# Sparse attention and two feed-forward layers on one core: v loaded 64 rows at a time into two buffers

## The chip, the core and the metric

The kernel runs on one core of a Trainium2 chip. TensorE (PE) multiplies matrices out of the on-chip memory into eight accumulator banks, VectorE (DVE), ScalarE (ACT) and GpSimd (POOL) do the element-wise work, and SyncE (SP) issues nearly all transfers between the chip's main memory and the on-chip memory. The engines run on their own and wait for each other by semaphores; each takes its own instructions strictly in order. The metric is the time of one execution in microseconds, as the device measures it.

## The reference

```
scores = q @ k.T / sqrt(64)                      # 4 batches, 8 heads, 576 positions
heads 0-3: keys with 0 <= i - j < 32             # local
heads 4-7: keys j <= i, j % 32 == i % 32         # strided
attn = exp(scores - max);  attn = attn / (sum(attn) + 1e-9)
x = attn @ v                                     # 2304 tokens, 512 wide
h = x @ w_in;   x = (h * sigmoid(1.702 h)) @ w_out      # 512 -> 2048 -> 512
h = x @ w2_in;  y = (h * sigmoid(h)) @ w2_out           # 512 -> 2048 -> 512
```

All inputs are float32, and so is the result.

## The kernel before

The 2304 tokens are cut into eight chunks c = 0 to 7 of 288 tokens, half a batch each. A chunk passes through `attention(c)` and then through the first feed-forward layer in `chunk(c)`. Chunk 7's first layer and the second layer for all tokens follow from 466 us on, under a plan of their own, which the change does not touch.

To use the fast 16-bit products and keep float32 accuracy, an operand is multiplied by a power of two (its scale) and split into a high and a low 16-bit half: the high half is made on ACT (L398) or POOL (L400), the low half on DVE (L405), and each product becomes three (`HI_LO`). A scale needs the sum of squares of its operand: squares are summed on ACT (L504) or DVE (L506) and added up over the partitions by a small product on PE (L419, `scale_sums`). Chunks 0 and 1 multiply q, k and v directly as float32; chunk 0 does its feed-forward so too (L846, L876), while the weights are still coming in.

The weights are 64-bit numbers in memory. `convert` brings in one of 16 blocks of `w_in` or `w_out` (512 KB, `conv_load`, L276), makes three passes on ACT (L444, L281, L285), one on DVE (L289) and one on POOL (L294), and only then can PE use the block. A small product on PE per block (L302) collects its norm. Chunk 0's products on f blocks 0 to 15 follow the blocks as they become ready, and chunk 1 starts when all 16 blocks of `w_out` are done.

For each chunk, `load_v` (L588) brings v into the tile `rv`: three transfers of 63 rows for the local heads into partitions 0 to 62, and for the strided heads either three of 54 rows (even c) or eleven of 18 to 54 rows with pieces of 1 KB (odd c) into partitions 64 and up. There is one `rv`. It is free again when chunk c has split it into `vz` (c > 1), or, for chunks 0 and 1, when their last product with v (L772) has run; the load of the next chunk waits for that on SP, with everything behind it in SP's order.

The softmax of a pair of heads, one local and one strided (`pair`, four per chunk), runs PE scores (L696) - DVE maximum and subtraction (L708, L710) - ACT exp (L713) - DVE sum and reciprocal (L716, L718) - POOL multiplication (L719) - PE transposition (L725) - ACT or DVE copy to `ptt` (L730 to L739). Its row of 64 score columns holds 63 scores, and the last column holds 1e-9 all the time, so that the sum over 64 columns is sum + 1e-9. Five places for the scores (`prt`, NSM), five for `ptt` (NPT), four for the chunk's outgoing tokens (`ts`, NTS, written by L823 and stored by SP at L826) and eight blocks for weights in work (`wm`, NF) are there.

Nothing of this order is found at run time. `Planner` plays the tasks through at build time with a cost for each, gives each engine the ready task of the lowest due time, and writes the instructions in the order of the starts it found. A transfer ends in that plan after a queue time at `rate` (0.27 MB per us here) and 2.0 us more. A buffer count, a cost or a landing time that is changed therefore moves instructions on every engine.

Of the kernel before, what the change touches and what calls it, by code (L numbers as in the profile page):

```python
# [61 lines left out]
class Planner:  # L62
# [32 lines left out]
    def run(self, t=0.0):  # L95
# [17 lines left out]
        while todo:  # L113
# [21 lines left out]
            for e in sorted(engines, key=lambda e: engines[e]):  # L135
# [35 lines left out]
                if isinstance(got.wait, tuple):  # L171
                    link = max(link, got.t1) + got.wait[1] / self.rate
                    end = link + 2.0
                else:
                    end += got.wait
# [8 lines left out]
def attention_moe_moe2_kernel(  # L184
# [133 lines left out]
    NV = 12  # L318
    rv = at.tile([128, NV, 4, D], F32, name="rv")
    qh = at.tile([128, 2, NQ + 16], F16, name="qh")  # L320
    kh = at.tile([128, 2, 2, NK], F16, name="kh")

    vz = at.tile([128, 2, NV * 4, D], F16, name="vz")
    NSM, NPT, NTS, NCV, NF = 5, 5, 4, 2, 8
    prt = at.tile([128, NSM, NLB, 2, W], F32, name="prt")
# [23 lines left out]
    def sel(t, pattern, base, cm):  # L349
        nc.gpsimd.affine_select(  # L350
            out=t, in_=t, pattern=pattern, compare_op=ALU.is_ge, fill=NEG,
            base=base, channel_multiplier=cm)

    nc.vector.memset(rep, 0.0)
    nc.vector.tensor_copy(out=rep[0:32].rearrange("p (j k) -> p j k", j=4), in_=idb[0:32, None, 0:32].to_broadcast([32, 4, 32]))
    nc.vector.memset(rv[0:W, 3 * NLB:NV], 0.0)
    nc.vector.memset(rv[32:W], 0.0)
    nc.scalar.activation(out=tot[:, 0, 0:1], in_=ones[:, 0:1], func=AF.Exp)
    nc.scalar.activation(out=rv[96:128].rearrange("p n h d -> p (n h) d"), in_=ones[96:128, None, 0:D].to_broadcast([32, 4 * NV, D]),
                         func=AF.Copy, scale=0.0)  # L360
# [3 lines left out]
    nc.gpsimd.memset(mk[0:32, 4, 0, 0:31], NEG)  # L364
    sel(mk[0:32, 0], [[0, NLB], [1, W]], 0, -1)
    sel(mk[0:32, 0], [[0, NLB], [-1, W]], 31, 1)
    for z, r, d in ((2, R9, 0), (3, R18, R9)):
# [5 lines left out]
    for i in range(2):  # L373
        nc.gpsimd.memset(rk[64:128, i, 0:KO], 0.0)
    nc.gpsimd.memset(qh[:, :, NQ:NQ + 16], 0.0)
    nc.gpsimd.memset(prt[:, :, :, :, W - 1], 1e-9)


    P = Planner({"ps": range(8), "rq": [0], "rk": range(2), "rv": [0], "qh": [0],
                 "k0": [0], "k1": [0], "vz": [0], "x1": [0], "sl": range(NSM), "pt": range(NPT), "t": range(NTS),  # L380
                 "cv": range(NCV), "f": range(NF)} | {f"g{f}": [0] for f in range(KF)}, 0.27)

# [189 lines left out]
    def attention(c, b):  # L572
        s = c % 2
        tab = ATT0 if c == 0 else ATT1 if c == 1 else ATT
        rqb, rvb = P.buf("rq"), P.buf("rv")

# [11 lines left out]
        def load_v(on):  # L588
            vc = v[c].rearrange("p i h d -> p i (h d)")
            to = rv.rearrange("p n h d -> p n (h d)")  # L590
            parts = [(0, slice(3 * j, 3 * j + 3), vc[32 * j + 1:32 * j + W, 0:NLB]) for j in range(3)]
            if s == 0:
                parts += [(W, slice(4 * z, 4 * z + 4), vc[27 * z:27 * z + 54, NLB:NLB + 4]) for z in range(3)]
            else:
                parts += [(W + R18 * u, slice(n, n + 7 * m - 6, 7),
                           vc[R18 * r:R18 * (r + w), NLB + i:NLB + i + 3 * m - 2:3])
                          for n, m, u, i, r, w in ((0, 2, 0, 0, 0, 3), (1, 2, 0, 0, 3, 3), (2, 1, 0, 0, 6, 1), (2, 1, 1, 1, 0, 2),
                                                   (3, 1, 0, 1, 2, 3), (4, 1, 0, 1, 5, 2), (4, 1, 2, 2, 0, 1), (5, 1, 0, 2, 1, 3),
                                                   (6, 1, 0, 2, 4, 3), (9, 1, 0, 4, 2, 3), (10, 1, 0, 4, 4, 3))]
            for p0, n0, x in parts:  # L600
                nc.sync.dma_start(out=to[p0:p0 + x.shape[0], n0], in_=x)
        kv = P.add({"SP": 0.4 + 0.5 * s}, b + tab["load"][1], load_v, (), [rvb], wait=("dma", 1.2))


        if c > 0:
            sq = [*([square(c, b + tab["square"][0], NQ, 0, lambda: rq, [kq], [rqb])] if c > 1 else []),
                  *[square(c, b + tab["square"][1], 128 * NV, 1 + 3 * z, lambda z=z: rv.rearrange("p b h d -> p (b h d)")[
                      :, 128 * NV * z:128 * NV * (z + 1)], [kv], [rvb]) for z in range(2)]]
# [27 lines left out]
        if c > 1:  # L636
            qhb, vzb = P.buf("qh"), P.buf("vz")
            k_q = hi_lo(b + tab["split"][0], NQ, lambda: qh[:, 0, 0:NQ], lambda: qh[:, 1, 0:NQ], lambda: rq, lambda: sc_t[c]["q"],
                        [k_sc], [qhb], [rqb])
            split_k(c, b + tab["split"][1])  # L640
            k_v = []
            for t in range(2):
                rvv = rv.rearrange("p b h d -> p (b h) d")[:, 2 * NV * t:2 * NV * (t + 1)]
# [10 lines left out]
        def pair(i):  # L654
# [6 lines left out]
            def scores(on):  # L661
# [45 lines left out]
            for g in range(2):  # L707
# [40 lines left out]
        def times_v(r):  # L748
# [4 lines left out]
            def mm(on):  # L753
                seq = [[], []]
                for g in range(2):
                    rows = slice(W * g, W * g + W)
                    for e, j, c0, n in BLOCKS[s] if g else [(e, j, 0, 0) for e in range(NLB) for j in range(3)]:
                        for x, (y, z) in enumerate(HI_LO if c > 1 else HI_LO[:1]):
                            for hh in range(2):
# [631 lines left out]
```

## Time and profile before

| | |
|---|---|
| median of 3 runs | 851.86 us (850.16 to 853.89) |
| profiled execution, its own time | 851.69 us |
| its span, first to last instruction | 849.9 us |
| PE busy | 814.9 us (96%) |
| DVE, ACT, POOL busy | 618.2, 530.4, 383.5 us |
| PE idle | 35.0 us, of it 25.4 before 125.3 us |
| moved by transfers | 156.83 MB, 185 GB/s |

Times in all rows are us from the span's start. A row of a timeline ends with the idle time of the engine just before it and what ended that. A granted clock of 1.00 is TensorE's upper level, 2.4 GHz, and 0.50 its lower, 1.2 GHz; 0.78 for a stretch is a mean of the two.

### The profile page before, as it was taken

What the parts mean: (1) busy time and instruction counts of PE and PEld (TensorE: products, weight loads), DVE (VectorE), ACT (ScalarE), POOL (GpSimd) and SP (SyncE); (2) the same over time, 40 slices, a digit from 0 to 9 for tenths busy, and PEclk for the clock granted to TensorE, in tenths of its full rate; (3) what the DMA queues carried; (4) which work ended last, traced back from release to release, by engine and by line L of the source; (5) the groups of instructions that cost most, each with busy time, mean ns of one, the idle gap of its engine ahead of it and who ended that gap; (6) DMA issues with size and microseconds to landing.
All of it is one profiled execution on the core that took longest, in us unless ns stands there. A gap on an engine that the chain in (4) does not pass through costs nothing.

```text
span 849.9 us, 24691 instructions
## 1 busy us (share of the span) xinstructions
PE 814.9 (96%) x10112; PEld 682.7 (80%) x10112; DVE 618.2 (73%) x1118; ACT 530.4 (62%) x980; POOL 383.5 (45%) x396
## 2 busy tenths in 40 slices
PE   4989889999999999999999999999999999999997
PEld 2766567877877878877788878888889988888886
DVE  5357679977786989978652537789888799878742
ACT  5788569569879788886761515455554676645510
POOL 4346755342432556734410543778877543211110
PEclk9999989999999999999999999999999999999999
DMA  8968443155474686663310743776666898657501
GB/s 230 267 217 276 121 125 107 39 164 190 140 221 151 216 288 196 197 220 122 109 45 24 305 163 109 234 230 223 224 212 219 299 295 306 235 173 231 180 26 50
DMA packets 90545, 156.83 MB, mean 185 GB/s; under 512 B 9096, under 2 KB 48848, under 8 KB 90432
## 3 DMA queue, kind: packets, MB, share of 16 engines
q1 hardware_dynamic: 90112, 154.67, 56.3%
q8 instruction: 79, 1.29, 0.7%
q10 hardware_dynamic: 320, 0.59, 0.3%
q14 instruction: 34, 0.28, 0.1%
HBM read 101.74 MB, written 53.48 MB: 183 GB/s over the span
## 4 chain that ended last, share of the span: by engine, by line
PE 68%; DMA 15%; DVE 5%; ACT 5%; POOL 3%; issue 2%; SPq 1%; DVEq 0%; POOLq 0%; ACTq 0%
PE aps L1161 10%; PE aps L1272 8%; DMA rv<-in_v_dram 7%; PE hps L1161 5%; PE aps L849 4%; PE gps L1161 4%; PE gps L880 4%; PE aps L880 4%; PE hps L1272 4%; PE gps L1272 4%; DMA regB<-in_moe_w_in_dram 2%; PE gps L849 2%; PE hps L880 2%; PE hps L849 2%; PE gps L1024 1%
## 5 line engine op out<-in xcount | busy, mean ns | idle before, releaser
L1161 PEld LDWEIGHTS <-wf 128*128 128x128 f16 x1680 | 150.6, 98 | 15.3
L1272 PEld LDWEIGHTS <-wf 128*128 128x128 f16 x1512 | 147.6, 98 | 18.6 <-issue 1.1
L849 PEld LDWEIGHTS <-regA 128*128 128x128 f16 x1152 | 112.5, 98 | 29.3 <-issue 0.3
L880 PEld LDWEIGHTS <-regB 128*128 128x128 f16 x1152 | 110.2, 98 | 26.7
L977 POOL TENSOR_TENSOR tt<-tt 128x256 f32<-128x256 f32 (+2 forms) x84 | 75.2, 905 | 45.4 <-ACT tt L1173 12.1
L849 PE MATMUL aps<-x,regA 128*128 128x288 f16 x624 | 83.0, 286 | 0.0
L294 POOL TENSOR_TENSOR wm<-wm 128x512 int32<-128x512 int32 x32 | 45.9, 1438 | 68.1 <-DVE wm L289 63.0
L972 ACT ACTIVATE wf<-tt,xsg 128x512 f16<-128x512 f32 x87 | 58.0, 713 | 26.0 <-PE hps L1272 6.7
L984 DVE SCALAR_TENSOR_TENSOR wf<-tt,xsg,wf 128x512 f16<-128x512 f32 x87 | 70.5, 857 | 0.0
L880 PE MATMUL aps<-g,regB 128*128 128x288 f16 x432 | 58.9, 286 | 0.0
L719 POOL TENSOR_TENSOR prt<-prt,sus 128x378 f32<-128x378 f32 x32 | 29.1, 916 | 55.6 <-DVE sus L718 50.0
L1272 PE MATMUL aps<-regA,wf 128*128 128x256 f16 x456 | 53.2, 273 | 0.1
L1161 PE MATMUL aps<-xfa,wf 128*128 128x256 f16 (+1 forms) x528 | 53.1, 256 | 0.0
L880 PE MATMUL gps<-g,regB 128*128 128x288 f16 x384 | 52.2, 286 | 0.0
L880 PE MATMUL hps<-g,regB 128*128 128x288 f16 x336 | 44.7, 286 | 0.0
L1173 ACT ACTIVATE tt<-tt 128x512 f32<-128x512 f32 x39 | 24.4, 625 | 30.5 <-DVE tt L1168 30.3
L849 PE MATMUL gps<-x,regA 128*128 128x288 f16 x288 | 39.2, 286 | 0.0
L1161 PE MATMUL aps<-g,wf 128*128 128x256 f16 x324 | 38.8, 273 | 0.0
L972 ACT ACTIVATE wf<-regB,xsg 128x512 f16<-128x512 f32 x39 | 26.8, 713 | 18.9 <-DMA regB<-g_scratch 5.9
L405 DVE SCALAR_TENSOR_TENSOR g<-aps,sg,g 128x288 f16<-128x288 f32 x52 | 26.2, 512 | 17.0 <-ACT g L398 16.7
L1272 PE MATMUL aps<-regB,wf 128*128 128x256 f16 x312 | 37.0, 273 | 0.0
L289 DVE SCALAR_TENSOR_TENSOR wm<-wm,aps 128x512 int32<-128x512 int32 x35 | 23.8, 681 | 15.5 <-ACT aps L285 15.5
(335 smaller groups left out, 1906.4 us busy)
## 6 DMA issues: line engine op xcount, KB each, us to landing
tt<-g_scratch SPq DMA_DIRECT2D x76, 256.0 KB
g_scratch<-tt SPq DMA_DIRECT2D x64, 256.0 KB
w<-in_moe_w_out_dram SPq DMA_DIRECT2D x24, 512.0 KB
regB<-in_moe_w_in_dram SPq DMA_DIRECT2D x16, 512.0 KB
w<-in_moe_w_in_dram SPq DMA_DIRECT2D x16, 512.0 KB
w_scratch<-wm SPq DMA_DIRECT2D x32, 256.0 KB
regB<-g_scratch SPq DMA_DIRECT2D x32, 256.0 KB
wf<-in_factors SPq DMA_DIRECT2D x8, 896.0 KB
```

The lines of the kernel that those rows point to most:

```text
L289: nc.vector.scalar_tensor_tensor(out=mi, in0=mi, scalar=3, in1=ri, op0=ALU.logical_shift_left, op1=ALU.bitwise_or)
L294: nc.gpsimd.tensor_tensor(out=di, in0=m.bitcast(I32), in1=di, op=ALU.add)
L405: dve_t(n), prio, lambda on: nc.vector.scalar_tensor_tensor(out=lo(), in0=src(), scalar=s(), in1=hi(), op0=ALU.mult, op1=ALU.subtract),
L719: kno = P.add({"POOL": 1.0}, t + 8, lambda on: nc.gpsimd.tensor_tensor(out=sets(N), in0=sets(N), in1=wide(sus[:, sl.idx], 2 * NLB), op=ALU ...
L849: nc.tensor.matmul(o, lhsT=pvA[:, f, x, kk, :], rhs=x1[:, y, kk, :], start=(i == 0), stop=(i == 3 * KD - 1))
L880: nc.tensor.matmul(o, lhsT=pvB[:, f, u, dt * 128:(dt + 1) * 128], rhs=g1[:, w, f, :], start=(f == 0 and j == 0), stop=(f == KF - 1 and j = ...
L972: nc.scalar.activation(out=out, in_=in_, func=AF.Copy, scale=s)
L977: return P.add({e: x for e, x in any_add(n).items() if e in by}, prio, lambda on: (nc.gpsimd if on == "POOL" else nc.vector).tensor_tensor ...
L984: dve_t(n), prio, lambda on: nc.vector.scalar_tensor_tensor(out=lo(), in0=src(), scalar=s(), in1=hi(), op0=ALU.mult, op1=ALU.subtract),
L1161: nc.tensor.matmul(place(b, f), lhsT=wf[:, nf * g + f, x, wa, 128 * kk:128 * kk + 128], rhs=rhs.rearrange("p (h t) -> p h t", h=2) if n2 = ...
L1173: return P.add(act_t(512), t + 5, lambda on: nc.scalar.activation(out=sl(b), in_=sl(b), func=AF.Silu), after, (), [b], tab="silu")
L1272: nc.tensor.matmul(bank(b)[:, 256 * half:256 * half + 256], lhsT=fb[:, x, a, 128 * f:128 * f + 128], rhs=wt[:, 4 * p + f, z, wi, :], start ...
```

## The change

Below, v2 is the load of v for chunk 2, and so on.

- `rv` becomes two buffers, `rv0` for even and `rv1` for odd chunks, each with its own place in the plan. v of chunk c+1 can be loaded while chunk c's is in use.
- The local loads, and the strided ones of even chunks, take 64 rows instead of 63 and 54. The additional rows carry values that meet a zero probability; the masks move by the one column. In odd chunks the eleven small transfers stay as they were.
- The scores take all 64 columns; the column with 1e-9 goes, and DVE adds 1e-9 to the six sums of a pair just before the reciprocal, 32 instructions more.
- NSM and NPT go from 5 to 4, NTS from 4 to 3, NF from 8 to 7.
- In the plan the queue rate goes from 0.27 to 0.30, a load of v costs SP 1.0 us (even) or 3.0 us (odd) instead of 0.4 and 0.9, and it lands 1.0 or 3.0 us later than its queue time says.
- At the start, DVE clears the last quarter of both buffers (2 x 768 elements) and the lower half of `rv1`; ACT's clearing of 32 rows and POOL's filling of the column go.

```diff
-                    end = link + 2.0
+                    end = link + 2.0 + sum(got.wait[2:])
...
-    rv = at.tile([128, NV, 4, D], F32, name="rv")
+    rv = at.tile([128, 2, NV, 4, D], F32, name="rv")
...
-    NSM, NPT, NTS, NCV, NF = 5, 5, 4, 2, 8
+    NSM, NPT, NTS, NCV, NF = 4, 4, 3, 2, 7
...
-    nc.vector.memset(rv[0:W, 3 * NLB:NV], 0.0)
-    nc.vector.memset(rv[32:W], 0.0)
+    nc.vector.memset(rv[0:W, :, 3 * NLB:NV], 0.0)
+    nc.vector.memset(rv[W:128, 1], 0.0)
     nc.scalar.activation(out=tot[:, 0, 0:1], in_=ones[:, 0:1], func=AF.Exp)
-    nc.scalar.activation(out=rv[96:128].rearrange("p n h d -> p (n h) d"), in_=ones[96:128, None, 0:D].to_broadcast([32, 4 * NV, D]),
-                         func=AF.Copy, scale=0.0)
...
-    nc.gpsimd.memset(prt[:, :, :, :, W - 1], 1e-9)
...
-    P = Planner({"ps": range(8), "rq": [0], "rk": range(2), "rv": [0], "qh": [0],
+    P = Planner({"ps": range(8), "rq": [0], "rk": range(2), "rv0": [0], "rv1": [0], "qh": [0],
...
-        rqb, rvb = P.buf("rq"), P.buf("rv")
+        rqb, rvb = P.buf("rq"), P.buf(f"rv{s}")
...
-            parts = [(0, slice(3 * j, 3 * j + 3), vc[32 * j + 1:32 * j + W, 0:NLB]) for j in range(3)]
+            parts = [(0, slice(3 * j, 3 * j + 3), vc[32 * j:32 * j + W, 0:NLB]) for j in range(3)]
             if s == 0:
-                parts += [(W, slice(4 * z, 4 * z + 4), vc[27 * z:27 * z + 54, NLB:NLB + 4]) for z in range(3)]
+                parts += [(W, slice(4 * z, 4 * z + 4), vc[27 * z:27 * z + W, NLB:NLB + 4]) for z in range(3)]
...
-        kv = P.add({"SP": 0.4 + 0.5 * s}, b + tab["load"][1], load_v, (), [rvb], wait=("dma", 1.2))
+        kv = P.add({"SP": 1.0 + 2.0 * s}, b + tab["load"][1], load_v, (), [rvb], wait=("dma", 1.2, 1.0 + 2.0 * s))
...
-            N = W - 1
+            N = W
...
-            krc = P.add({"DVE": 0.15}, t + 5.1, lambda on: nc.vector.reciprocal(out=sus[:, sl.idx], in_=sus[:, sl.idx]), [ku], (), [sl])
+
+            def inverse(on):
+                nc.vector.tensor_scalar(out=sus[:, sl.idx], in0=sus[:, sl.idx], scalar1=1e-9, scalar2=None, op0=ALU.add)
+                nc.vector.reciprocal(out=sus[:, sl.idx], in_=sus[:, sl.idx])
+            krc = P.add({"DVE": 0.22}, t + 5.1, inverse, [ku], (), [sl])
```

First place: SP's transfers while the weights come in. `regB<-in_moe_w_in` and `regB<-in_moe_w_out` are blocks of weights; `rv` of three and three rows belongs to an even chunk, the one with the small pieces to an odd one. Before, from the blocks 8 to 11 of `w_in` on:

```order
L276 DMA regB<-in_moe_w_in_dram 128x1024 x4
L601 DMA rv<-in_v_dram 63x768 x3
L601 DMA rv<-in_v_dram 54x2x256 x2
L601 DMA rv<-in_v_dram 18x256
L601 DMA rv<-in_v_dram 36x256
L601 DMA rv<-in_v_dram 54x256
L601 DMA rv<-in_v_dram 36x256
L601 DMA rv<-in_v_dram 18x256
L601 DMA rv<-in_v_dram 54x256 x4
L276 DMA regB<-in_moe_w_in_dram 128x1024 x4
L276 DMA regB<-in_moe_w_out_dram 128x1024 x6
```

After, from the end of the load of v1 on:

```order
L598 DMA rv<-in_v_dram 54x256 x4
L276 DMA w_103<-in_moe_w_out_dram 128x1024 x2
L576 DMA rq<-in_q_dram 64x1152
L577 DMA rq<-in_q_dram 64x1152
L276 DMA regB<-in_moe_w_in_dram 128x1024 x4
L598 DMA rv<-in_v_dram 64x768 x3
L598 DMA rv<-in_v_dram 64x1024 x3
L276 DMA regB<-in_moe_w_in_dram 128x1024 x4
L276 DMA regB<-in_moe_w_out_dram 128x1024 x7
```

The load of v1 has moved up past six blocks of weights and q of chunk 1, and v2, which stood behind the 13th block of `w_out`, now stands between blocks 11 and 12 of `w_in`.

Second place: DVE where v2 is squared (`jv,tot<-rv`). Before, among the low halves of `w_in` (L405), late in chunk 0's feed-forward:

```order
L405 SCALAR_TENSOR_TENSOR regA<-regA,s 128x512
L800 SCALAR_TENSOR_TENSOR x_75<-aps,x1s,x_75 128x288 x2
L405 SCALAR_TENSOR_TENSOR regA<-regA,s 128x512
L289 SCALAR_TENSOR_TENSOR wm<-wm,gps 128x512
L405 SCALAR_TENSOR_TENSOR regA<-regA,s 128x512 x2
L506 SCALAR_TENSOR_TENSOR jv,tot<-rv 128x1536
L405 SCALAR_TENSOR_TENSOR regA<-regA,s 128x512
L257 TENSOR_SCALAR a<-aps 128x3
L259 TENSOR_SCALAR t<-a 128x3
L263 RECIPROCAL s<-t 128x3
```

After, where the last blocks of `w_in` are converted (`wm<-wm` is L289, `nms` and `prt` belong to chunk 1's softmax):

```order
L289 SCALAR_TENSOR_TENSOR wm<-wm,hps 128x512
L705 TENSOR_REDUCE nms<-hps 128x3
L705 TENSOR_REDUCE nms<-gps 128x3
L707 TENSOR_TENSOR prt<-hps,nms 128x3x64
L707 TENSOR_TENSOR prt<-gps,nms 128x3x64
L503 SCALAR_TENSOR_TENSOR jv,tot<-rv 128x1536
L289 SCALAR_TENSOR_TENSOR wm<-wm,hps 128x512
L503 SCALAR_TENSOR_TENSOR jv,tot<-rv 128x1536
L289 SCALAR_TENSOR_TENSOR wm<-wm,gps 128x512
L733 TENSOR_SCALAR ptt<-aps 128x384
```

The square that was one instruction on DVE and one on ACT is now two on DVE, and two conversions stand behind and between them.

Third place: SP after v of chunk 3. `x_scratch<-ts` are the stores of chunk 0's outgoing tokens, `rk` is k for chunks 4 and 5. Before:

```order
L601 DMA rv<-in_v_dram 54x256 x4
L826 DMA x_scratch<-ts 128x288 x3
L562 DMA rk<-in_k_dram 64x1280
L563 DMA rk<-in_k_dram 64x1152
L826 DMA x_scratch<-ts 128x288 x2
L276 DMA w_103<-in_moe_w_in_dram 128x1024
```

After:

```order
L598 DMA rv<-in_v_dram 54x256 x4
L559 DMA rk<-in_k_dram 64x1280
L560 DMA rk<-in_k_dram 64x1152
L598 DMA rv<-in_v_dram 64x768 x3
L598 DMA rv<-in_v_dram 64x1024 x3
L559 DMA rk<-in_k_dram 64x1280
L560 DMA rk<-in_k_dram 64x1152
L827 DMA x_scratch<-ts 128x288 x5
L276 DMA w_103<-in_moe_w_in_dram 128x1024
```

The load of v4 and both loads of k now stand ahead of the first store.

## Rows read from the trace of the kernel before

**Rows 1.** The page: busy time of each engine, and TensorE's granted clock in 40 slices.
```profile
PE 814.9 (96%) x10112; PEld 682.7 (80%) x10112; DVE 618.2 (73%) x1118; ACT 530.4 (62%) x980; POOL 383.5 (45%) x396
PEclk9999989999999999999999999999999999999999
```

**Rows 2.** Busy time by stretch: length, five engines, granted clock, DMA share, GB/s.
```profile
0.00:79.70 79.70, 63.28 (x840) 48.18 (x840) 40.67 (x97) 58.14 (x105) 36.12 (x50) 0.98 0.84 241
79.70:109.70 30.00, 21.48 (x182) 15.79 (x182) 20.92 (x29) 19.16 (x33) 20.67 (x15) 0.94 0.57 168
109.70:125.30 15.60, 15.10 (x125) 11.76 (x126) 14.17 (x18) 11.88 (x16) 10.55 (x7) 0.78 0.39 113
125.30:500.00 374.70, 370.70 (x5667) 298.45 (x5666) 282.57 (x586) 268.65 (x539) 157.43 (x153) 1.00 0.50 164
500.00:850.00 350.00, 344.38 (x3302) 308.48 (x3300) 259.86 (x391) 172.53 (x289) 158.75 (x173) 1.00 0.60 198
```

**Rows 3.** Waits of TensorE up to 130 us: total us, times, longest us.
```profile
PE hps L302 <- POOL regB L294: 5.9, 3, 2.8
PE aps L772 <- DMA rv<-in_v_dram: 5.6, 3, 4.3
PE aps L419 <- ACT jk L504: 2.6, 1, 2.6
```

**Rows 4.** Timeline, 108 to 111 us: start, us, instruction, [idle before <- releaser].
```profile
108.11 1.48 ACT L504 ACTIVATE jk<-rv 128x1536 uint8<-128x1536 f32 x1 [3.83 <-DMA rv<-in_v_dram]
108.82 1.76 DVE L506 SCALAR_TENSOR_TENSOR jv<-rv 128x1536 uint8<-128x1536 f32 x1 [3.64 <-DMA rv<-in_v_dram]
109.73 0.45 PE L419 MATMUL aps<-tot,ones 128*128 128x1 f32 x2 [2.64 <-ACT jk L504]
110.65 0.58 PE L419 MATMUL aps<-tot,ones 128*128 128x1 f32 x2 [0.46 <-DVE jv L506]
```

**Rows 5.** Timeline of SyncE's transfers up to 130 us.
```profile
37.24 15.87 SPq L601 DMA_DIRECT2D rv<-in_v_dram  x14
53.20 1.77 SPq L276 DMA_DIRECT2D regB<-in_moe_w_in_dram  x4
95.96 2.17 SPq L601 DMA_DIRECT2D rv<-in_v_dram  x6
```

**Rows 6.** The chain of waits up to 130 us: start, us, what.
```profile
9.73 13.50 DMA rv<-in_v_dram
97.76 11.04 DMA rv<-in_v_dram
```

**Rows 7.** Busy time by stretch, while 64-row loads of q and k run.
```profile
74.40:82.40 8.00, 6.23 (x107) 4.45 (x107) 7.02 (x7) 4.70 (x10) 5.38 (x5) 1.00 0.97 255
```

**Rows 8.** Timeline of TensorE, 62 to 66 us.
```profile
62.17 0.61 PE L302 MATMUL hps<-regA 128*128 128x128 bf16 x4 [2.09 <-POOL regA L294]
62.57 3.63 PE L846 MATMUL gps<-x,regA 128*128 128x288 f32 x8
```

**Rows 9.** Timeline of GpSimd, 64 to 88 us.
```profile
64.66 2.50 POOL L294 TENSOR_TENSOR regA<-wm,regA 128x512 int32<-128x512 int32 x2 [0.38 <-DVE wm L289]
79.62 8.34 POOL L294 TENSOR_TENSOR regB<-wm,regB 128x512 int32<-128x512 int32 x4 [1.90 <-DVE wm L289]
```

**Rows 10.** A small VectorE operation: min/median/max ns.
```profile
L264 DVE TENSOR_SCALAR s<-s x13: 153/169/666, 61.5 to 520.1; 128x1 f32<-128x1 f32 x5, 128x3 f32<-128x3 f32 x4, 128x2 f32<-128x2 f32 x4
```

**Rows 11.** Instructions on rv, min/median/max ns.
```profile
L506 DVE SCALAR_TENSOR_TENSOR jv<-rv x7: 1711/1758/2423, 54.1 to 366.2; 128x1536 uint8<-128x1536 f32 x7
L356 DVE MEMSET rv<- x1: 698/698/698, 1.2 to 1.2; 64x768 f32 x1
```

**Rows 12.** Timeline of VectorE, 135 to 137 us.
```profile
135.27 1.97 DVE L405 SCALAR_TENSOR_TENSOR kh<-rk,s,kh 128x1280 f16<-128x1280 f32 x1
```

**Rows 13.** The chain of waits at 690 us.
```profile
690.38 3.50 DMA g_scratch<-tt
```

**Rows 14.** Waits of TensorE, 130 to 500 us.
```profile
PE aps L725 <- POOL prt L719: 2.7, 3, 1.4
```

More of the change, by code (lines that the diff above doesn't have):

```diff
@@ L363, in attention_moe_moe2_kernel @@
     nc.gpsimd.memset(mk[0:32, 3, :, 54:W], NEG)
-    nc.gpsimd.memset(mk[0:32, 4, 0, 0:31], NEG)
-    sel(mk[0:32, 0], [[0, NLB], [1, W]], 0, -1)
-    sel(mk[0:32, 0], [[0, NLB], [-1, W]], 31, 1)
+    nc.gpsimd.memset(mk[0:32, 4, 0, 0:32], NEG)
+    sel(mk[0:32, 0], [[0, NLB], [1, W]], -1, -1)
+    sel(mk[0:32, 0], [[0, NLB], [-1, W]], 32, 1)
     for z, r, d in ((2, R9, 0), (3, R18, R9)):
@@ L375, in attention_moe_moe2_kernel @@
     nc.gpsimd.memset(qh[:, :, NQ:NQ + 16], 0.0)
-    nc.gpsimd.memset(prt[:, :, :, :, W - 1], 1e-9)
-    P = Planner({"ps": range(8), "rq": [0], "rk": range(2), "rv": [0], "qh": [0],
+    P = Planner({"ps": range(8), "rq": [0], "rk": range(2), "rv0": [0], "rv1": [0], "qh": [0],
                  "k0": [0], "k1": [0], "vz": [0], "x1": [0], "sl": range(NSM), "pt": range(NPT), "t": range(NTS),
-                 "cv": range(NCV), "f": range(NF)} | {f"g{f}": [0] for f in range(KF)}, 0.27)
+                 "cv": range(NCV), "f": range(NF)} | {f"g{f}": [0] for f in range(KF)}, 0.30)
     def start(n):
@@ L589, in load_v @@
             vc = v[c].rearrange("p i h d -> p i (h d)")
-            to = rv.rearrange("p n h d -> p n (h d)")
-            parts = [(0, slice(3 * j, 3 * j + 3), vc[32 * j + 1:32 * j + W, 0:NLB]) for j in range(3)]
+            to = rv[:, s].rearrange("p n h d -> p n (h d)")
+            parts = [(0, slice(3 * j, 3 * j + 3), vc[32 * j:32 * j + W, 0:NLB]) for j in range(3)]
             if s == 0:
-                parts += [(W, slice(4 * z, 4 * z + 4), vc[27 * z:27 * z + 54, NLB:NLB + 4]) for z in range(3)]
+                parts += [(W, slice(4 * z, 4 * z + 4), vc[27 * z:27 * z + W, NLB:NLB + 4]) for z in range(3)]
             else:
@@ L601, in load_v @@
                 nc.sync.dma_start(out=to[p0:p0 + x.shape[0], n0], in_=x)
-        kv = P.add({"SP": 0.4 + 0.5 * s}, b + tab["load"][1], load_v, (), [rvb], wait=("dma", 1.2))
+        kv = P.add({"SP": 1.0 + 2.0 * s}, b + tab["load"][1], load_v, (), [rvb], wait=("dma", 1.2, 1.0 + 2.0 * s))
         if c > 0:
             sq = [*([square(c, b + tab["square"][0], NQ, 0, lambda: rq, [kq], [rqb])] if c > 1 else []),
-                  *[square(c, b + tab["square"][1], 128 * NV, 1 + 3 * z, lambda z=z: rv.rearrange("p b h d -> p (b h d)")[
+                  *[square(c, b + tab["square"][1], 128 * NV, 1 + 3 * z, lambda z=z: rv[:, s].rearrange("p b h d -> p (b h d)")[
                       :, 128 * NV * z:128 * NV * (z + 1)], [kv], [rvb]) for z in range(2)]]
@@ L642, in attention @@
             for t in range(2):
-                rvv = rv.rearrange("p b h d -> p (b h) d")[:, 2 * NV * t:2 * NV * (t + 1)]
+                rvv = rv[:, s].rearrange("p b h d -> p (b h) d")[:, 2 * NV * t:2 * NV * (t + 1)]
                 z = [vz[:, a, 2 * NV * t:2 * NV * (t + 1)] for a in range(2)]
@@ L678, in scores @@
                                     o = LQ * e + 32 * j
-                                    seq[0].append((L[32 * j:32 * j + 32, W * e:W * e + W - 1], qx[:, o:o + 32], kx[:, o + 1:o + W], last))
+                                    seq[0].append((L[32 * j:32 * j + 32, W * e:W * e + W], qx[:, o:o + 32], kx[:, o:o + W], last))
                                 continue
@@ L767, in mm @@
                                     o, pt, u = o[:, LQ * e + 32 * j:LQ * e + 32 * j + 32], pt[:, m:m + 32], 3 * j + e
-                                seq[g].append((o, vz[rows, y, 4 * u + h, :] if c > 1 else rv[rows, u, h, :], pt, x == 0, x == 2 or c < 2))
+                                seq[g].append((o, vz[rows, y, 4 * u + h, :] if c > 1 else rv[rows, s, u, h, :], pt, x == 0, x == 2 or c < 2))
                 for n in range(0, max(len(x) for x in seq), 2):
```

## The prediction

> **What bounds the kernel now.** I read the page first: PE is busy 814.9 of 849.9 us, so 35.0 us is all that idle time can give, and a lower clock is the only other loss [rows 1]. The second look was the busy time by stretch [rows 2]. It splits the idle time: 16.4 us up to 79.7, 8.5 from there to 109.7, 0.5 up to 125.3, 4.0 up to 500 and 5.6 behind. From 125.3 to 500 us PE is 99% busy at the full clock, and what remains behind 500 is not touched by the change. So the case is decided before 125.3 us, while the weights come in. The granted clock is 0.94 in the second stretch and 0.78 in the third; the missing 6% of 30.0 us and 22% of 15.6 us are 1.8 and 3.4 us that PE lost there at the lower level, next to 9.0 us of idle time. The stretch from 79.7 to 125.3 thus holds 14.2 us that PE does not need.
>
> Third I read who ended PE's waits [rows 3]: 5.9 us for converted blocks of w_out, 5.6 for the first load of v, 2.6 for a square on ACT, the last at one place. The timeline there [rows 4] shows what the reader is to see: ACT stood 3.83 us and DVE 3.64 us, both for v2; behind their squares PE waited 2.64 and 0.46 us for the scale of chunk 2. That is 3.1 us in which ready products of chunk 0 stood behind the scale product in PE's order, and right behind it the clock was low: 3.4 us more. v2 had been issued only at 95.96 [rows 5], and the chain gives 11.04 us of its time to it [rows 6].
>
> **The change, part by part.** The sum is made against the profiled execution's own 851.69 us (849.9 us of span and 1.8 around it), 0.2 us under the median.
>
> *v2 early.* With a second buffer and its new place v2 goes out between blocks 11 and 12 of w_in, ahead of the four blocks that went out at 53.20, so some 43 us sooner [rows 5], since its buffer is free once chunk 0's products are done. DVE now squares it among the last conversions of w_in, and nothing waits for it at 104 us. That removes 3.1 us of wait and the low clock behind it, 3.4 us: 6.5 us. What is late next there is the conversion of w_out, for which PE waited 5.9 us elsewhere in the stretch; those waits I leave as they are. Bounds: 3.1 us if another pause at this place brings the clock down all the same, 14.2 us if the conversions, no longer held up by ACT's and DVE's stand, run ahead of PE through the whole stretch.
>
> *v2 ahead of weights.* Blocks 12 to 15 of w_in now land behind v2, and PE already waited 2.09 us for block 12 and then ran at the lower clock (eight products in 3.63 us) [rows 8]. v2 is 3 x 192 KB + 3 x 256 KB = 1.38 MB. The nearest row for 64-row loads is the stretch in which q and k of chunks 2 and 3 come in, 255 GB/s at a DMA share of 0.97 [rows 7]: 5.4 us. Against it stands the better shape of the first load: the chain waits 13.50 us for it [rows 6], while up to 79.7 us the queue moved 241 GB/s [rows 2]. If all that goes before block 12 moves at 255, it is through 5.5% sooner, 3.4 us of 62. That leaves +2.0 us, and I take it; the bounds are 0 (the first load's gain is as large as its price) and 5.4 (it gains nothing).
>
> The row that speaks for 255 GB/s is a stretch of loads of 64 rows that keep the engines 0.97 busy. The Trainium skill, "SBUF — State Buffer", section "Door 1: The DMA port swizzle", says that 64 partitions reach only 8 of the 16 ports on the memory's side, and gives 196 GB/s for them. By that figure, an estimate, v2 costs 7.0 us instead of 5.4 and the sum is 1.6 us worse. The trace's 255 GB/s is above the page's figure, so the row decides.
>
> *Squares next to conversions.* Two squares of v2 on DVE at 1.76 us [rows 11] now run while POOL converts the last blocks of w_in. One conversion on POOL takes 1.25 us alone and 2.09 us where DVE squares q and k: two in 2.50 us, four in 8.34 [rows 9]. Three conversions (blocks 10 to 12) at 0.84 us more are 2.5 us. The squares also stand in DVE's order ahead of blocks 11 and 12; behind them wait the conversions of these blocks, POOL's additions and PE's products on them. But PE is then waiting for block 12 anyway, which lands behind v2: the two prices overlap, and I add nothing for this one, with 0 and 2.5 us as ends.
>
> The rows show POOL at 2.09 us against 1.25. The Trainium skill, "SBUF — State Buffer", section "Who interferes with whom", makes it harder: a VectorE instruction with two inputs in this memory and a GpSimd instruction that reads it hold a shared interface one at a time, and the second one waits for the whole of the first. By that rule each square could cost a conversion its full 1.76 us, 3.5 us in all, and if none of it overlapped the forecast would be that much later. Rows of before do not show so much.
>
> *v1 early, v0 faster.* v1's fourteen transfers took SP 15.87 us and held up blocks 12 to 15 of w_in, issued at 53.20 [rows 5]; now they stand ahead of blocks 8 to 11 too. Their 1.2 MB are 4.7 us at 255 GB/s; less 5.5% of some 43 us, 2.4, that is 2.3 us later. PE then comes to block 12, which waits behind v2 in any case: I take 0, from 0 to 2.3. PE's 5.6 us wait for v0 [rows 3] shrinks, but what PE wins there it waits again at block 12: 0, with -5.6 as the end.
>
> *The rest.* 32 additions on DVE at 0.17 us [rows 10] are 5.4 us over some 400 us, beside PE's work and on an engine busy 73% of the span: 0, at most 0.5. One score column more, and 378 elements becoming 384, are under 2% of operations that end nothing. The start has one more clearing of 0.70 us [rows 11] ahead of PE's first product, hidden in the wait for v0; without that cover, 0.7 us. Four softmax places are as many as a chunk has pairs; PE waited 2.7 us in all for a normalised pair from 130 to 500 us [rows 14]. I take no change, -2.7 to +3.
>
> Sum: 851.7 - 6.5 + 2.0 = 847.2 us. On the median's scale that is 847.4.
>
> **The rivals.**
>
> *Given back.* PE arrives earlier and waits for the next late thing, the blocks of w_out (5.9 us of waits already [rows 3]) or block 12. For it: POOL was busy 20.7 of 30.0 us from 79.7 on [rows 2], and what chunk 2 needs (high and low halves of q, k, v) now falls into that same stretch. Against it: ACT and DVE stood still for 3.7 us exactly there. If v2 costs its full 5.4 us, 851.7 - 6.5 + 5.4 = 850.6; 850 to 853.
>
> *Slower: stores behind loads.* The stores of chunk 0's tokens now stand on SP behind v4 and the second load of k, which waits until DVE has made the low half of the k before it (1.97 us at 135.27 [rows 12]). There are three `ts` places for four columns of tokens, so ACT's fourth copy waits for a store to land; 3.50 us is one store's time [rows 13]. Behind that copy stand ACT's gelus and high halves, and PE runs out of banks. For it: the order, and the fourth place is gone in all seven chunks of this plan. Against it: in the order ACT has nine operations between the first copy and the fourth. If each chunk lost half a store's time, 1.75 us, it is 7 x 1.75 = 12.3 us, and 847.2 + 12.3 = 859.5; from 0.65 us a chunk on it takes back the whole 4.5 us. I put it at 856 to 860.
>
> *More than the wait.* With ACT and DVE never stopped, w_out's conversions finish ahead of PE, and most of the 14.2 us closes: with 2.0 us of price, 839.5; 838 to 843. Against it: POOL's load in that stretch.
>
> **How the numbers follow.** Forecast 0.50 (own range 845 to 851, since its cost may be 0 to 5.4), given back 0.20, slower 0.13, more 0.17. Anything within 0.5% (4.3 us) is about what a measurement of this kernel cannot tell from no change, so faster means under 847.6. A little over half of the forecast's chance lies there, 0.29, and all of the last rival's: 0.46. The rest of the forecast and the giving back are the same: 0.41. Slower 0.13. The range goes from 840 to 855: it leaves out the lower end of the largest gain and the slower rival.
>
> **What would show it.** In the profile after: no wait of ACT, DVE or PE for v around 104 to 110 us, no low clock behind it, and chunk 1's first 16-bit products (L849 before) starting some 4 us before 125.3. v2 issued before 60 us. PE's wait for block 12 of w_in longer by about 2 us, and POOL's additions of blocks 11 to 13 near 2 us. From there to 500 us PE 99% busy. I am wrong if PE's wait for blocks of w_in grows by more than 5 us, if the time from 79.7 us to chunk 1's start stays at 45 us, or if new waits of PE stand beside stores of `ts` behind 125 us.

## The result and the profile after

The changed kernel takes 857.5 us, median of 6 runs (854.4 to 858.9), against 851.0 for the kernel before in the runs beside it (848.8 to 853.9, 6 runs). The ratio is 1.0071, with a 95% interval of 1.0046 to 1.0096: some 6 us slower. I had forecast 847.4 in a range of 840 to 855 and given "slower" 0.13. The profiled execution of after took 857.71 us, 6.0 more than that of before.

The same rows of the page of after; they answer to [rows 1]:

```profile
PE 820.3 (96%) x10112; PEld 684.6 (80%) x10112; DVE 619.6 (72%) x1144; ACT 528.3 (62%) x981; POOL 390.5 (46%) x395
PEclk9989999999999999999999999999999999999999
```

PE is 5.4 us longer busy, and its idle time is the same (35.3 us). More busy time for nearly the same products means lower clock, so idle time and clock have to be read together, by stretch. The busy time by stretch of after, which answers to [rows 2]:

```profile
0.00:79.70 79.70, 64.89 (x744) 49.16 (x745) 42.32 (x101) 54.25 (x100) 35.36 (x46) 0.94 0.87 254
79.70:109.70 30.00, 25.71 (x282) 18.89 (x280) 26.91 (x39) 22.80 (x41) 26.26 (x19) 0.94 0.66 192
109.70:125.30 15.60, 13.16 (x137) 9.74 (x138) 14.64 (x24) 10.33 (x16) 12.30 (x9) 1.00 0.75 188
125.30:500.00 374.70, 366.52 (x5608) 293.77 (x5606) 273.54 (x589) 267.91 (x536) 155.30 (x149) 1.00 0.48 154
```

Idle time plus the share lost to the clock, before and after:

| stretch | before | after | difference |
|---|---|---|---|
| 0 to 79.7 us | 16.4 + 1.6 = 18.0 | 14.8 + 4.8 = 19.6 | +1.6 |
| 79.7 to 125.3 | 9.0 + 5.2 = 14.2 | 6.7 + 1.8 = 8.5 | -5.7 |
| 125.3 to 500 | 4.0 + 0 = 4.0 | 8.2 + 1.7 = 9.9 | +5.9 |

(The 1.7 of the last row is half of 3.41 us at the lower level, too short to show in the two digits of its clock.) That is 1.8 of the 6.0 us. Up to 3.0 more lie at the very start, where these two traces record no clock, before 28.0 us in one and 30.0 us in the other. The timeline of TensorE of after shows the level there by the length of eight equal products:

```profile
26.11 4.08 PE L847 MATMUL aps<-x,regA 128*128 128x288 f32 x8
30.26 2.16 PE L847 MATMUL hps<-x,regA 128*128 128x288 f32 x8
```

Before, the first eight of them started at 28.97 us and took 2.15 us. Of the runs below, sq5_behind_ts has the same start as after, and its trace does record the level there. Behind 3.4 us at the upper level, the busy time by stretch shows a granted clock of 0.50:

```profile
13.80:30.70 16.90, 14.02 (x197) 11.71 (x198) 8.17 (x18) 12.30 (x24) 9.69 (x9) 0.50 1.02 286
```

If the level was the lower one all the way up to the recorded part, after did 20.7 us of work at it and before 14.7, and half of the difference is 3.0 us. The last 1.2 us I can't assign.

So the gain that I forecast is there (-5.7), and two losses stand against it: one up to 80 us, larger than forecast, and one behind 125 us, where I had said that nothing would change. The waits of TensorE in after, up to 130 us and then from 130 to 500 us, answer to [rows 3, 14]:

```profile
PE hps L302 <- POOL regB L294: 6.7, 7, 2.1
PE hps L661 <- DVE rep L355: 6.5, 1, 6.5
PE aps L661 <- ACT g L855: 2.8, 1, 2.8
PE gps L693 <- DMA rq<-in_q_dram: 1.0, 1, 1.0
...
PE hps L693 <- DMA rq<-in_q_dram: 0.9, 1, 0.9
PE aps L302 <- POOL regA L294: 0.8, 1, 0.8
PE aps L773 <- DMA rv<-in_v_dram: 0.3, 2, 0.2
...
PE gps L850 <- ACT ts L824: 2.2, 1, 2.2
PE hps L693 <- issue: 2.1, 1, 2.1
```

The 5.6 us for v0 are down to 0.3, the 2.6 us for a square of v2 are gone. New are 1.9 us for q of chunk 1, 2.8 us for a bank that ACT empties only behind its pass over block 12 of w_in, 2.2 us for a copy to `ts` and 2.1 us for scores.

The pause of 2.2 us is the largest piece behind 125 us, and the low clock (142.6 to 146.1 us) follows it. The timelines of SyncE, ScalarE and TensorE of after around it:

```profile
134.18 0.47 SPq L559 DMA_DIRECT2D rk<-in_k_dram  x1
135.38 7.10 SPq L827 DMA_DIRECT2D x_scratch<-ts  x4
...
139.70 1.27 ACT L501 ACTIVATE jk<-rk 128x1280 uint8<-128x1280 f32 x1 [1.15 <-DMA rk<-in_k_dram]
140.97 0.48 ACT L395 ACTIVATE g<-aps,sg 128x288 f16<-128x288 f32 x1
141.35 0.49 ACT L395 ACTIVATE g<-gps,sg 128x288 f16<-128x288 f32 x1
141.73 0.41 ACT L824 ACTIVATE ts<-gps 128x288 f32<-128x288 f32 x1
...
142.19 2.64 PE L850 MATMUL gps<-x,regA 128*128 128x288 f16 x12 [2.20 <-ACT ts L824]
```

PE wants the bank that ACT's fourth copy of chunk 0's tokens empties. ACT stands 1.15 us for k of chunk 5 (call it k5), issued only at 134.18, squares it, makes two high halves, and only then copies. But the copy also needs one of three `ts` places, and the first store, issued at 135.38 behind k5, landed at 141.15. The copy started at 141.73, so two causes end 0.6 us apart, and the trace names only the later one. That called for experiments on each alone and on both.

### The profile page after: what moved, and what is told of

Its sections match the earlier page's. It is cut to its first block, busy times and chain, and to the rows that moved or that the text cites. A ratio compares the mean times of both kernels' runs of the same rounds, so it can differ in the third digit from the quotient of the medians.

```text
span 855.6 us, 24711 instructions
## 1 busy us (share of the span) xinstructions
PE 820.3 (96%) x10112; PEld 684.6 (80%) x10112; DVE 619.6 (72%) x1144; ACT 528.3 (62%) x981; POOL 390.5 (46%) x395
## 4 chain that ended last, share of the span: by engine, by line
PE 61%; DMA 11%; DVE 11%; ACT 8%; POOL 4%; issue 3%; SPq 1%; DVEq 0%; ACTq 0%; POOLq 0%
PE aps L1162 10%; PE aps L1273 8%; PE hps L1162 5%; PE gps L1162 4%; PE hps L1273 4%; PE gps L1273 4%; PE aps L850 3%; PE hps L881 3%; DMA rv<-in_v_dram 3%; DMA rq<-in_q_dram 2%; PE aps L881 2%; PE gps L881 2%; PE hps L850 2%; PE gps L850 2%; POOL wm L294 2%
## 5 line engine op out<-in xcount | busy, mean ns | idle before, releaser
L294 POOL TENSOR_TENSOR wm<-wm 128x512 int32<-128x512 int32 x32 | 48.2, 1507 | 83.7 <-DVE wm L289 78.9
L881 PE MATMUL aps<-g,regB 128*128 128x288 f16 x576 | 78.5, 286 | 0.0
L850 PE MATMUL aps<-x,regA 128*128 128x288 f16 x552 | 74.5, 288 | 0.0
L720 POOL TENSOR_TENSOR prt<-prt,sus 128x384 f32<-128x384 f32 x32 | 29.2, 917 | 46.7 <-DVE sus L718 34.5
L850 PE MATMUL hps<-x,regA 128*128 128x288 f16 x336 | 45.6, 286 | 0.5 <-DVE g L402 0.5
L402 DVE SCALAR_TENSOR_TENSOR g<-aps,sg,g 128x288 f16<-128x288 f32 x46 | 23.1, 512 | 24.1 <-ACT g L395 24.0
L850 PE MATMUL gps<-x,regA 128*128 128x288 f16 x264 | 36.8, 291 | 2.2 <-ACT ts L824 2.2
L294 POOL TENSOR_TENSOR regA<-wm,regA 128x512 int32<-128x512 int32 x16 | 21.6, 1359 | 32.1 <-DVE wm L289 31.1
```

The lines of the kernel that those rows point to most:

```text
L294: nc.gpsimd.tensor_tensor(out=di, in0=m.bitcast(I32), in1=di, op=ALU.add)
L402: dve_t(n), prio, lambda on: nc.vector.scalar_tensor_tensor(out=lo(), in0=src(), scalar=s(), in1=hi(), op0=ALU.mult, op1=ALU.subtract),
L850: nc.tensor.matmul(o, lhsT=pvA[:, f, x, kk, :], rhs=x1[:, y, kk, :], start=(i == 0), stop=(i == 3 * KD - 1))
L881: nc.tensor.matmul(o, lhsT=pvB[:, f, u, dt * 128:(dt + 1) * 128], rhs=g1[:, w, f, :], start=(f == 0 and j == 0), stop=(f == KF - 1 and j = ...
```

## The experiments

Several edits move single instructions of the finished plan and leave all others in their order:

```diff
+        for k, to in self.moves:
+            k.t0 = to.t0 + 1e-3
         for k in sorted(self.tasks, key=lambda k: (k.t0, k.seq)):
             k.fn(k.on)
```

Ratios are to the kernel before, on the same chip; the changed kernel itself has 1.0071.

**The square of k5 behind the fourth copy.**

```diff
+                if x == 5:
+                    P.moves.append((sq[-1], ts_copy))      # the last of chunk 0's copies
```

> One instruction moves against the changed kernel: ACT's square of k of chunk 5 (127 lines of order below nothing else) stands behind ACT's fourth copy of chunk 0's tokens instead of three places ahead of it. Theory A (ACT was held by this square, whose load was issued only at 134.18 us): the high halves and the copy no longer wait for that load, PE's pause of 2.20 us at 142 us and the 3.41 us at the lower clock behind it (1.7 us lost) go: 857.5 - 3.9 = 853.6 us. Rival B (three ts places): the fourth copy needs the first store to have landed, which the trace has at 141.15 us against 141.73 for the copy, so it gains 0.6 us at most and the clock falls all the same: 856.9 to 857.5.

**A fourth ts place.** Its room comes from an unused row of `mk`.

```diff
-    NSM, NPT, NTS, NCV, NF = 4, 4, 3, 2, 7
+    NSM, NPT, NTS, NCV, NF = 4, 4, 4, 2, 7
```

> The changed kernel with a fourth ts place (room for it comes from an unused row of the masks); every engine's order is that of the changed kernel. Rival B (stores behind loads, three places): the pauses beside ts copies go, at 142 us 2.2 us and 1.7 us of clock, and what other chunks lose: 853.6 us or less. Theory A (the square of k of chunk 5 ends last): the copy at 141.73 us stays where it is: 857.5, within 0.5 us.

**Both.**

> Both edits in one: the square of k of chunk 5 behind the fourth copy, and four ts places. If each of the two alone would hold the copy to about 141 us (theory AB: square and store overlap), only this one gains, 3.9 us: 853.6. Theory A and rival B alone say the same here, 853.6; they differ in the two single runs. If PE then waits for the next late thing (the gelus of chunk 1 or a bank), 855 to 857.

Measured: 1.0056 (1.0031 to 1.0081), 1.0071 (1.0039 to 1.0103) and 1.0026 (1.0003 to 1.0049). The rows that decide are ACT's, in this order: the square moved (first row), four places (second and third), both (the last two).

```profile
138.85 0.41 ACT L828 ACTIVATE ts<-gps 128x288 f32<-128x288 f32 x1 [1.84 <-DMA x_scratch<-ts]
```

```profile
136.38 1.27 ACT L501 ACTIVATE jk<-rk 128x1280 uint8<-128x1280 f32 x1 [1.99 <-DMA rk<-in_k_dram]
138.41 0.41 ACT L824 ACTIVATE ts<-gps 128x288 f32<-128x288 f32 x1
```

```profile
137.22 0.42 ACT L828 ACTIVATE ts<-gps 128x288 f32<-128x288 f32 x1
138.67 1.27 ACT L503 ACTIVATE jk<-rk 128x1280 uint8<-128x1280 f32 x1 [1.04 <-DMA rk<-in_k_dram]
```

With the square out of the way the copy waits for a store; with a fourth place it stands behind the square, which waits for k5; with both it waits for neither. PE's pause at this copy is 1.67 us in the first, 3.04 in the second, and gone in the third, where a pause of 0.37 us for something else is all that is left. It is there in the three runs below that keep the order of after at this place (1.96 to 2.96 us), and in none of the four that have both edits. Theory A and rival B were each half right: the two causes overlap. The pair is worth about its price, forecast as 3.9 us and 0.45% or 3.8 us by the two ratios, whose intervals just touch. That neither edit is enough alone is shown by these rows; the ratios don't separate the moved square alone from the pair.

**q of chunk 1 ahead of v1.** `if c == 1: P.moves.append((kv, kq))`

> Against the changed kernel only SP's order moves: the two transfers of q of chunk 1 (and the two of w_out ahead of them) go out before the fourteen of v of chunk 1, not behind them. Theory: PE's waits of 0.86 and 0.99 us at 42 to 44 us and the 3.41 us at the lower clock behind them (1.7 us lost) go, 3.1 us by the lag of PE's work there: 857.5 - 3.1 = 854.4. Rival (given back at block 12): PE arrives earlier at block 12 of w_in, which still lands behind v of chunk 2 at 59.6 us, and waits there what it gained: 857 to 858, with that wait 2.8 us longer by some 3 us.

1.0092 (1.0063 to 1.0120). The waits for q are gone, and the rival holds at another block: PE waits 3.98 us at block 8 of w_in, and 5.26 us at a block of w_out. The blocks of w_in stood behind v1 before this edit too, and block 8 landed only 1.0 us later than in after. But v1 itself lands later, and ACT and DVE wait 5.21 and 8.95 us for it to square it, with conversions behind the squares (the waits of TensorE from 40 to 130 us, then ACT's row).

```profile
PE hps L304 <- POOL regB L296: 9.1, 7, 5.3
PE aps L304 <- POOL regA L296: 4.7, 2, 4.0
```

```profile
43.63 1.48 ACT L503 ACTIVATE jk<-rv 128x1536 uint8<-128x1536 f32 x1 [5.21 <-DMA rv<-in_v_dram]
```

**v2 behind block 15 of w_in, and its squares later.** Two forms, the second with the squares alone:

```diff
+        if c == 2:
+            P.moves.append((kv, loads[15]))                # only in the first
+                P.moves.extend((x, bits[17]) for x in sq[1:3])
```

> Against the changed kernel the six transfers of v of chunk 2 go out behind block 15 of w_in, not ahead of block 12, and DVE's two squares of it stand behind the bits of the first block of w_out; nothing else moves. Theory (bytes ahead of weights and squares ahead of blocks 11 and 12): the 2.80 and 0.81 us that PE waits from 58 to 63 us shrink to the 2.1 us of the kernel before and half of the low clock's 6.83 us goes; by the lag of PE's work there (+2.6 us between 57 and 69 us) 857.5 - 2.6 = 854.9. Rival (given back): the blocks of w_out land behind the same bytes either way, PE waits for them instead between 80 and 93 us: 857 to 858.

> Against the changed kernel only DVE's two squares of v of chunk 2 move, behind the bits of the first block of w_out; the loads stay. What the prediction took (squares next to conversions cost nothing, since block 12 is late anyway): 857.5, within 0.7. Rival (DVE's order held block 11 for 3.4 us and block 12 for 1.8): PE's wait at 58 us (2.80) shrinks by 1 to 2.8 us: 855 to 856.5.

1.0069 (1.0037 to 1.0100) and 1.0082 (1.0053 to 1.0111). Neither tells what it should: at their new place the squares stood ahead of DVE's part of the scale of w_in, and PE waited 4.32 and 2.40 us for that scale. The squares did not wait for v2 here; their own work, 1.75 and 2.70 us, was enough. Squares at a third place, behind that of q of chunk 2, with both edits of the ACT pair in, and then v1 moved as well:

```diff
+                P.moves.extend((x, sq[0]) for x in sq[1:3])
...
+        if c == 1:                                         # only in the second
+            P.moves.append((kv, loads[11]))
+                P.moves.extend((x, bits[12]) for x in sq[0:2])
```

> The kernel of sq5_ts4 (measured 852.8), and v of chunk 2 issued behind block 15 of w_in, with DVE's two squares of it behind the square of q of chunk 2, where the scale of w_in no longer stands behind them (in v2_behind_win PE waited 4.32 us at 71 us for that scale). Theory (v of chunk 2 ahead of the weights costs what PE waits from 56 to 62 us): the lag of PE's work there falls by 4 to 7 us and stays so: 846 to 849. Rival (given back): PE comes earlier to the blocks of w_out, which land behind the same bytes in either order, and waits for them between 80 and 93 us: 851.5 to 854.

> As v2_after_weights, and v of chunk 1 issued behind block 11 of w_in (its place in the kernel before), with ACT's and DVE's squares of it behind the bits of block 12. Theory (every load of v ahead of weights costs PE its landing time): the waits at 41 to 44 us go too, another 1 to 3 us: 844 to 848. Rival (given back at w_out): 851 to 854, with the waits for blocks of w_out from 80 us on longer than 5.9 us by what was won.

1.0055 (1.0032 to 1.0077), and 1.0093 (1.0067 to 1.0118) with v1 behind block 11 as well. Again the squares came with a pause of their own, 8.18 us of PE in the first, this time since one of them waits for its load: DVE waited 4.48 us for q of chunk 2, then squared q and v2, and only then made the bits for which POOL and PE waited. I did not look for what makes the second slower still.

```profile
86.22 0.61 PE L304 MATMUL hps<-regB 128*128 128x128 bf16 x4 [8.18 <-POOL regB L296]
```

```profile
78.81 1.36 DVE L507 SCALAR_TENSOR_TENSOR jv<-rq 128x1152 uint8<-128x1152 f32 x1 [4.48 <-DMA rq<-in_q_dram]
80.21 1.76 DVE L507 SCALAR_TENSOR_TENSOR jv<-rv 128x1536 uint8<-128x1536 f32 x1
82.01 1.76 DVE L507 SCALAR_TENSOR_TENSOR jv<-rv 128x1536 uint8<-128x1536 f32 x1
83.69 0.68 DVE L291 SCALAR_TENSOR_TENSOR wm<-wm,hps 128x512 int32<-128x512 int32 x1
```

So the last pair puts the squares where DVE waits anyway, right ahead of the square of q of chunk 2: first the squares alone, then the load too, by the line above.

```diff
+            if c == 2:
+                P.moves += [(sq[1], sq[0]), (sq[2], sq[0]), (sq[0], sq[2])]
```

> The kernel of sq5_ts4 (852.8), and DVE's two squares of v of chunk 2 stand right ahead of the square of q of chunk 2, where DVE waited 2.74 us for that load; all loads stay. Theory (DVE's order, not the bytes: the squares wait for v of chunk 2 and hold blocks 11 and 12 of w_in): the wait of 1.95 us at 57 us and the low clock behind it go, 849 to 851. Rival (bytes: block 12 lands at 59.6 us all the same): 852.5 to 853.5, with the wait at 57 to 60 us as long as before.

> As v2_squares_gap, and v of chunk 2 issued behind block 15 of w_in. In v2_after_weights the squares stood behind the square of q of chunk 2, which lands at 78.8 us, and held the bits of a block of w_out: PE waited 8.18 us. Theory (v of chunk 2 ahead of weights costs 4 to 7 us, and nothing later takes it back): 846 to 849. Rival (given back): whatever is won at block 12 is waited for again at the blocks of w_out from 78 to 93 us, since their loads stand behind the same bytes and DVE's and POOL's work is the same: 852 to 855.

1.0050 (1.0026 to 1.0073) and 1.0035 (1.0011 to 1.0059), against 1.0026 with v2 ahead of the weights: no gain. The waits of TensorE from 40 to 125 us, in sq5_ts4 and then in v2_after_weights_gap, show why:

```profile
PE hps L304 <- POOL regB L296: 7.1, 5, 2.8
PE aps L665 <- ACT g L861: 1.9, 1, 1.9
PE aps L304 <- POOL regA L296: 1.8, 3, 1.1
```

```profile
PE hps L304 <- POOL regB L296: 10.3, 6, 3.5
PE aps L304 <- POOL regA L296: 0.8, 2, 0.5
PE hps L304 <- ACT aps L287: 0.7, 1, 0.7
```

The waits at blocks of w_in (those for regA, and the one at L665, whose bank ACT empties only behind its pass over block 12) fall from 3.7 to 0.8 us; those for w_out (regB) rise by 3.9 with ACT's. The two executions are compared by their waits and not by their times: that of v2_after_weights_gap, 849.11 us, is the fastest of its twelve, and between 32 and 840 us its clock fell once, against twice. So the waits are given back, as the rival said. This points to the conversion of the blocks of w_out as what sets PE's pace up to 125 us, with PE paying the difference either earlier or later.

**Parts of the change alone.** The 64-row transfers, the 64th column and the additions, with one buffer, the old counts and the old planner's numbers:

```diff
-    rv = at.tile([128, 2, NV, 4, D], F32, name="rv")
+    rv = at.tile([128, 1, NV, 4, D], F32, name="rv")
-    NSM, NPT, NTS, NCV, NF = 4, 4, 3, 2, 7
+    NSM, NPT, NTS, NCV, NF = 5, 5, 4, 2, 8
...
-        kv = P.add({"SP": 1.0 + 2.0 * s}, b + tab["load"][1], load_v, (), [rvb], wait=("dma", 1.2, 1.0 + 2.0 * s))
+        kv = P.add({"SP": 0.4 + 0.5 * s}, b + tab["load"][1], load_v, (), [rvb], wait=("dma", 1.2))
```

> The changed kernel with one buffer for v, the old counts of places (5, 5, 4 and 8) and the old planner's numbers; what is left of the change is the 64-row transfers, the 64th score column and the constant added to the sums. SP's order is that of the kernel before. Theory (the start): PE's 5.6 us of waiting for v of chunk 0 goes, but 2 us are given back since the clock rises only some 2 us later than PE now starts its steady work: before - 1 = 850. Rival (nothing is given back): before - 4 = 847. Rival (the start does not count, PE waits for block 12 of w_in): 851, as before.

The other three are the line of counts of the change alone on the kernel before; the planner's numbers alone (its queue rate of 0.30, SP's costs and the landing times of v) on the kernel before; and the changed kernel with 0.27 and the last pair of lines above:

> The kernel before with the new counts of places alone: 4 softmax places and 4 for transposes instead of 5, 3 ts places instead of 4, 7 staging places instead of 8. What the prediction took: 851, -2.7 to +3. Rival (the places bring the loss): 855 to 858, with pauses of PE beside ts copies.

> The kernel before, planned with the new numbers alone: 0.30 for the queue's rate, 1 to 3 us more landing time for v and more of SP for its issue. Theory (the numbers only matter with the second buffer): 850 to 853. Rival (they move the loads of v and k so that ACT waits for a square as at 139 us of the changed kernel): 855 to 858.

> The changed kernel, planned with the old numbers: 0.27 for the queue's rate, no extra landing time for v, SP's old cost of a load. Theory (the second buffer and the places bring the loss, whatever the planner's numbers): 855 to 859. Rival (the new numbers bring it): 850 to 852, with k of chunk 5 landed before ACT comes to its square.

| run | ratio | 95% interval |
|---|---|---|
| rows64_one_buffer | 0.9991 | 0.9971 to 1.0012 |
| fewer_places | 0.9995 | 0.9977 to 1.0014 |
| new_planner_numbers | 1.0074 | 1.0043 to 1.0104 |
| old_planner_numbers | 1.0125 | 1.0091 to 1.0160 |

Transfers of 64 rows cost and give nothing, nor do the places. The planner's numbers alone make the kernel before as slow as the whole change does, and without them the two buffers are slower still. The profile of new_planner_numbers shows one form of it, the same as at 142 us of after: ACT waits for a load that it is to square, with a copy to `ts` behind it (ACT's rows), and PE waits for that copy. The busy time by stretch (last two rows) shows where both plans lose, new_planner_numbers first: PE is idle for 10.5 and 13.9 us from 125.3 to 500 us, against 4.0 before [rows 2].

```profile
129.49 1.16 ACT L504 ACTIVATE jk<-rq 128x1152 uint8<-128x1152 f32 x1 [2.52 <-DMA rq<-in_q_dram]
130.65 0.39 ACT L823 ACTIVATE ts<-aps 128x288 f32<-128x288 f32 x1
```

```profile
PE aps L849 <- ACT ts L823: 2.0, 1, 2.0
PE gps L849 <- ACT ts L823: 0.9, 1, 0.9
```

```profile
125.30:500.00 374.70, 364.24 (x5659) 292.23 (x5658) 281.56 (x577) 269.11 (x532) 152.14 (x148) 1.00 0.53 166
125.30:500.00 374.70, 360.82 (x5422) 287.32 (x5423) 264.19 (x572) 260.53 (x521) 155.28 (x146) 0.99 0.46 146
```

The 2.9 us at these copies are less than half of what new_planner_numbers loses there; the rest, and the 13.9 us of old_planner_numbers, I did not take apart. No run changes the order at random, so whether the planner's numbers themselves are to blame, or any order as far from that of before, stays open. Two runs came out over 3 us slower than anything expected of them: weights_first at 859.3 us and old_planner_numbers at 862.4.

No run points to a version that beats both kernels; the lowest ratio of the two-buffer ones is that of sq5_ts4.

## Why the prediction was wrong, point by point

The forecast was -4.5 us, and the two profiles give +6.0, 10.5 us apart. Of these, 5.9 lie behind 125.3 us, up to 2.6 before 79.7 us (measured 1.6 and up to 3.0, forecast +2.0), 0.8 in between, and 1.2 are not assigned.

- *v2 early, -6.5.* Right in place and about in size. The wait of 2.64 and 0.46 us for the scale product and the 6.83 us of low clock at 109.9 are gone, and the stretches from 79.7 to 125.3 us lose 5.7 us less. Chunk 1's first 16-bit product starts at 121.87 us against 125.25. Not right was "those waits I leave as they are": from 92 us on PE waits 4.6 us for blocks of w_out, where before it was 1.4.
- *v2 ahead of weights, +2.0.* The delay was about right: block 12 landed at 59.59 us against 56.41, block 15 at 63.27 against 61.59, so 3.2 and 1.7 us later. PE's waits there went from 2.09 to 3.61 us, and the low clock from 3.41 to 6.83: +3.2 in this pair of profiles, inside the bounds of 0 to 5.4. But it is not a price that can be saved: with the load behind the weights the waits moved to w_out.
- *Squares next to conversions, 0.* The overlap holds: moving the squares alone (v2_squares_gap) gave nothing. POOL slowed by DVE, which I looked at, came about as forecast (two conversions beside the squares took 3.96 us), but was not what mattered in the three other placements. There the squares held whatever stood behind them in DVE's order: twice by their own work, with 2.40 and 4.32 us for PE, and once because the square of q ahead of them waited for its load, with 8.18 us.
- *v1 early, 0; v0 faster, 0.* v0's wait fell from 5.6 to 0.3 us, as said. That it came to nothing was right by another path than mine, the wait at block 12: PE does its first products at the lower clock, and the clock rises 2.0 us later than before. In rows64_one_buffer, which has this faster load too, nothing was gained either (0.9991). q of chunk 1, which stood behind v1, cost 1.9 us that I had not named.
- *Behind 125.3 us, 0.* This is the step that failed. "From there to 500 us PE 99% busy" was the forecast; it is 97.8% (366.5 of 374.7), and 5.9 us more are lost than before, clock included. My third sign of being wrong, new waits of PE beside stores of `ts`, is what the profile shows. My slower rival had the place (stores behind the load of k, three `ts` places, the fourth copy) but not the second half, the square of k5 in ACT's order, and it priced half a store's time in each of seven chunks, 12.3 us; it happened once and was worth 3.9 (2.2 of wait, 1.7 of clock). The rest are shorter pauses, named below.
- *The rest, 0.* The counts were right (0.9995). Wrong was that I gave the planner's numbers no term. I read in the new order only where the loads of v had gone, and took the rest as the old order with shifts. They alone, on the kernel before, are worth 1.0074. The additional clearing at the start did cost its 0.7 us: PE's first product waits 6.49 us against 5.82, since the wait for v0 that was to cover it is gone.

What stays open: with the pair of edits 0.26% (0.03 to 0.49) is left. In that profile PE is busy 368.0 of 374.7 us from 125.3 on against 370.7 before, so it lies there, in nine pauses of 0.2 to 2.1 us: two at feed-forward products, seven at scores, normalised pairs and products with v. The largest is the L693 one above, which the other runs with after's plan have too (1.8 to 2.1 us in those named first). The profile shows nothing that ends there, and its cause stays open.

## What to carry to other kernels

When a planner's costs change, price the whole new order and not the part that the costs were meant for: on each in-order engine look for an instruction that waits for a load and stands ahead of one that frees a bank or a buffer. Where two causes end within a microsecond of each other, taking one away can show next to nothing; take both away before dropping either. And a wait in front of a stage is a gain only if nothing behind it in the same stage is due at the same time: here everything that came earlier at w_in was waited for again at w_out.

## What the runs showed of the hardware that I had not expected

- The stretches of low clock differ between profiles of the same order. After and ts4 have the same instructions in the same order but for one buffer; after has the lower level at 43.7, 60.7 (6.83 us), 88.0 and 142.6 us, ts4 at 59.9, 90.6, 138.4 and 350.0. Eight runs of ts4 spread from 851.2 to 861.4 us. The 3.4 us of low clock that I counted from a single profile was one draw.
- Loads of 64 rows alone in the queue moved at nearly the 255 GB/s of [rows 7] in one place and at less in another. In that stretch of before, q and k have the queue nearly to themselves up to 80.0 us, where a block of w_out follows. In after, the last four of v4's six transfers (0.98 MB) have it. Before first, then after:

```profile
74.40:80.00 5.60, 5.22 (x100) 3.57 (x99) 4.62 (x6) 2.32 (x5) 2.98 (x4) 1.00 0.96 250
121.30:125.80 4.50, 4.50 (x35) 3.48 (x33) 3.54 (x14) 3.52 (x5) 2.07 (x3) 1.00 0.90 218
```

  Averaged from 119 to 127 us, the rate of after would be 154 GB/s and the share 0.65, but next to nothing moves there for 0.8 us from 120.5 on and for the last 1.2 us. So a rate has to be taken from a stretch without gaps. By 218 GB/s v2's 1.38 MB would be 6.3 us and not 5.4, an estimate.
